# Rebuilding the opening of a fused attention and mixture-of-experts kernel

## The chip, the cores and the metric

The kernel runs on one core of a Trainium2 chip. The metric is the device time of one execution in microseconds (us), the median of several runs. Times inside an execution come from one profiled execution and count from the start of its span.

## What is computed

Causal attention over 8 batches with 8 heads of 576 positions and 64 dimensions, with a bias from a cumulative sum of `max(s, 0)`; its output, as 4608 rows of 512, goes through a layer of eight experts, one expert for each row, chosen by cosine similarity.

```python
scores = q @ k.T / sqrt(64)                       # per batch and head
cum    = cumsum(maximum(s, 0))
scores = where(causal, -1e9, scores + minimum(-(cum[:, None] - cum[None, :]), 0))
attn   = softmax(scores);  o = attn @ v
x      = o as [4608, 512]
e      = argmax(normalize(x) @ normalize(expert_emb).T / tau);  g = softmax(...)[e]
out    = g * (relu(x @ w1[e]) @ w2[e])
```

## The kernel before

The 64 heads are numbered n = 0 to 63, in groups g of four (`HG`) and batches of eight. All instructions are placed by hand, in program order, on each engine's own in-order queue; the only order between engines is what data and buffers demand. `step(n)` places one head's turn.

A softmax needs the maximum of each row ahead of the exponential. The kernel gets it from a first, rougher product: TensorE computes scores with `smax_mm` (1600 columns a head), VectorE takes the maxima. That work is in four parts: `s1` (tile i = 3, 448 columns), `s2` (tiles 2 and 1, 320 and 192), `s3` (half of tile 4, 288) and `s4` (the other half and tile 0, 288 and 64), with the reductions `sr(n, 3)`, `sr(n, 2)`, `sr(n, 1)`, one inside `s3` and two inside `s4`. In the steady state the same work has the names `s1`, `sa`, `s3`, `sb`. Its PSUM tiles are two banks named `s` (`ps_s`, two buffers); each allocation takes the other one, and has to wait until the one before on that bank has been read. Heads below 4 take theirs from `ps_t` for `s1` and `s2`.

The maxima of two heads (`MP`, 128 x 10) become a row: `mrow2` transposes them on TensorE, VectorE negates and shifts them, and a DMA on SyncE's queue (`send`) writes them into row 96 of the group's Q tile `qkb`. `mrow1` only queues that for the next step's pop of `rq`. With that row in place the exact scores need no subtraction.

The exact scores of head n go into two PSUM tiles, `ta` (placed by `ta_`) and `tb` (by `tb_` and `tbl`), by a high product (`hh_`, line 452) and a low one (`hl_`, line 456). The low one reads `QC` and `KC`, which hold for each head what is left of q and k after rounding: `neg` (line 324) and `hcopy` (line 318) on ScalarE write a negated and a plain copy of `qkb`, each for two heads, and `addl` (line 332) adds the unrounded values with an accumulating DMA on POOL's queue. `expa` and `expb1` (ScalarE, lines 489 and 492) take the exponentials; `pl_` (POOL, line 246) makes their low halves `PL`.

V is transposed by `emm` (line 293) through one PSUM tile of one buffer, and split into a high half on ScalarE (`vcp`, line 303) and a low half on VectorE (line 304). `vsq` (line 274) and `vscale` find V's scale for a batch. `pv(n)` (lines 517 to 519) multiplies the probabilities of head n with V two steps later, and `norm1` to `norm3` (lines 530 to 542) divide by the row sums a step after that. The experts follow behind head 63.

Loads: `load(g)` brings a group's q and k (1216 KB, POOL's queue) into one of three `qkb` tiles, `loadc` its rows of the cumulative sum, `zeros` and `onerows` fill the tile's other rows; `loadt` brings V (SyncE's queue).

The opening: steps -4 to -1 do the maxima of heads 0 to 3 with filler matmuls (`heat`, line 200) between them, steps 0 and 1 score heads 0 and 1 while they do the maxima of heads 4 to 6 (`m = n + LA` with `LA` = 5 from step 1 on), and from step 2 each step does the maxima of head n + 5. `prep(n, k)` gives each step two copies or negations on ScalarE for the next groups.

```python
m = n + LA - (n < 1)              # line 993: the head whose maxima step n does
if n == 0:                        # line 1129
    nc.sync.dma_start(cumd..., chl...)
    loadc(2); setup4(); load(2)
if n == 1:                        # line 1081, cut
    vscale(0); fslot(); ...; emm(0); s1(LA); s2(LA); ...
    vcp(0, False); vcp(0, True); prep(1, True); s3(LA); emm(1); s4(LA); mrow1(LA)
```

Of the kernel before, what the change touches and what calls it, by code (L numbers as in the profile page):

```python
# [110 lines left out]
def main(ctx, tc, qkh, qkc, vtin, s_in, emb, tau, w1h, w2h, out, shared, nb):  # L111
# [33 lines left out]
    chl = P32s[2][0:64, 0:2 * S].rearrange("p (x s) -> p x s", x=2).bitcast(F32R)  # L145
# [25 lines left out]
    def zeros(i):  # L171
        w = (QW + KW) // 4
        for j in range(4):
            nc.gpsimd.memset(qkbs[i][64:128, w * j:w * j + w].bitcast(F32), 0.0)
        onerows(i)
# [80 lines left out]
    def loadc(g):  # L256
        if g == 1:
            for i in range(2):
                nc.gpsimd.dma_start(qkbs[1][64 + i:65 + i, QW:].bitcast(F32), chl[HG:2 * HG, i, :].bitcast(F32))
        elif 1 < g < NGg:  # L260
# [73 lines left out]
    def prep(n, k):  # L334
# [3 lines left out]
        if g == 0:  # L338
            if c == 0:
                neg(1, False, 1 - k)  # L340
            elif c < 3:
                hcopy(1, k, c - 1)
            if c < 3:
                return
# [4 lines left out]
        else:  # L349
            hcopy(g + 1, k, c - 1)  # L350

# [13 lines left out]
    def stile(n, name):  # L365
        if n < LA - 1:
# [69 lines left out]

    def mrow2(j):
# [23 lines left out]
    def ta_(n):  # L461
# [3 lines left out]
        if n > 1:  # L465
            s1(n + LA)
# [525 lines left out]
    def step(n):  # L992
        m = n + LA - (n < 1)
# [4 lines left out]
        if m == 0:  # L998
# [3 lines left out]
            for i in range(2):  # L1002
# [5 lines left out]
                if i == 0:  # L1008
                    load(1)
                    zeros(1)  # L1010
                    loadc(1)
            setup2()
            zeros(2)
        if n < 0 and rq:
            rq.popleft()()
            aq.popleft()()
            for p in range(2):
                loadt(0, pair(p))
        if m == 2:
            setup3()  # L1020
        if m == 3:
            r7s[0]()
        if n == 0:
            neg(1, True, 0)
            neg(1, True, 1)
            addl(1, True)
# [9 lines left out]
        if not live or n < 2:  # L1036
            s1(m)
# [4 lines left out]
        if n == 1:  # L1042
            addl(1, False)
# [5 lines left out]
        if live:  # L1049
            expa(n)  # L1050
            if n != 1:
                prep(n, True)
# [9 lines left out]
        if live:  # L1062
            tb_(n)
        sr(m, 2)
        if n < 2:
# [15 lines left out]
        if n == 1:  # L1081
            vscale(0)
            fslot()
            while tasks:
                slot()
            emm(0)
            s1(LA)
            s2(LA)
            for i in (3, 2, 1):
                sr(LA, i)  # L1090
            vcp(0, False)
            vcp(0, True)
            prep(1, True)
            s3(LA)
            emm(1)
            s4(LA)
            mrow1(LA)
# [385 lines left out]
```

## Time and profile before

| | |
|---|---|
| median of 3 runs | 769.9 us (769.21 to 770.17) |
| the profiled execution | 770.33 us, of which its span 768.3 us |
| TensorE busy | 743.2 us (97%) |
| ScalarE, VectorE, POOL busy | 570.8, 525.1, 383.5 us |
| `ta` of head 0, 3, 9 starts | 21.52, 45.65, 74.96 us |

The page gives shares over the whole span; the opening has other limits than what follows. So the opening is read from the timeline of each engine, where each row is one instruction or a run of equal ones, with its start, its duration and, in brackets, how long the engine stood idle ahead of it and whose work ended that. Durations of neighbouring instructions overlap; where a rate is meant, the distance between starts is taken.

### The profile page before, as it was taken

To read this page: it belongs to the slowest core of one execution; us is meant where nothing else is said; L and a number is where in the kernel's file an instruction comes from. 1 tells how busy PE (TensorE), PEld (TensorE's weight loads), DVE (VectorE), ACT (ScalarE), POOL (GpSimd) and SP (SyncE) were. 2 spreads that over 40 slices of the span, in tenths; PEclk is the share of its full clock that TensorE was granted. 3 is DMA by queue.
4 is the path that set the end of the run, shared out by engine and by line. 5 is a ranking of instruction groups with operands and counts; after the bars stand their busy time and mean duration, and the time that the engine had idled before them with its cause. 6 is when DMAs were issued, how large, how long until landed. Compare 5 with 4: busy or idle time off the path is not lost. (4 is left out here: it accounts for less than half of the span.)

```text
span 768.3 us, 22128 instructions
## 1 busy us (share of the span) xinstructions
PE 743.2 (97%) x8587; PEld 550.2 (72%) x8587; DVE 525.1 (68%) x1794; ACT 570.8 (74%) x1024; POOL 383.5 (50%) x371
## 2 busy tenths in 40 slices
PE   7799999999999999999899999999999999999996
PEld 3599999999999999997464545645655555555564
DVE  7677888888888888889567666655665567645621
ACT  7789999999999999988676877738548578474410
POOL 8957798989899898774622130131221302211002
PEclk9889999999999999999999999999999999999999
DMA  8977879797979798854645965654665756643001
GB/s 157 228 175 146 173 181 206 175 216 167 211 170 214 168 206 176 209 168 156 196 150 178 185 192 168 153 194 112 166 199 114 191 168 174 210 106 88 15 15 57
DMA packets 76965, 125.46 MB, mean 163 GB/s; under 512 B 38981, under 2 KB 39385, under 8 KB 75986
## 3 DMA queue, kind: packets, MB, share of 16 engines
q0 software_dynamic: 20288, 71.07, 39.0%
q1 hardware_dynamic: 56564, 52.84, 25.6%
q8 instruction: 75, 1.23, 0.7%
q14 instruction: 38, 0.31, 0.1%
HBM read 95.38 MB, written 21.49 MB: 152 GB/s over the span
## 5 line engine op out<-in xcount | busy, mean ns | idle before, releaser
L246 POOL TENSOR_TENSOR PL<-P 128x576 f16<-128x576 f32 (+2 forms) x128 | 203.6, 1687 | 26.3 <-ACT P L489 15.5
L852 PEld LDWEIGHTS <-wt 128*128 128x128 f16 x1920 | 113.9, 98 | 87.3 <-issue 3.5
L852 PE MATMUL pxs<-xH,wt 128*128 128x512 f16 (+2 forms) x544 | 156.4, 359 | 1.8 <-PEq L901 1.0
L942 POOL DMA_INDIRECT out<-Kx,xj x39 | 41.5, 1064 | 174.6 <-DVE Kx L941 158.1
L725 POOL DMA_INDIRECT Qx<-xs,idx x41 | 42.5, 1036 | 128.1 <-ACT vjunk L807 74.6
L517 PE MATMUL om<-vh,P 128*128 128x73 f16 x945 | 105.1, 199 | 0.7 <-DVE xt L542 0.4
L518 PE MATMUL om<-vl,P 128*128 128x72 f16 x945 | 104.5, 196 | 0.0
L519 PE MATMUL om<-vh,PL 128*128 128x73 f16 x945 | 104.3, 197 | 0.0
L354 PE MATMUL s<-qkb 96*128 96x288 f32 (+4 forms) x270 | 97.0, 373 | 2.0 <-DVE M L362 1.1
L852 PE MATMUL T<-xH,wt 128*128 128x64 f16 x704 | 97.5, 193 | 0.0
L518 PEld LDWEIGHTS <-P 128*128 128x128 bf16 x960 | 94.7, 99 | 1.4 <-issue 1.0
L517 PEld LDWEIGHTS <-P 128*128 128x128 bf16 x960 | 93.6, 98 | 0.9 <-DVE vl L304 0.7
L519 PEld LDWEIGHTS <-PL 128*128 128x128 f16 x960 | 93.8, 98 | 0.0
L852 PE MATMUL pxs<-xL,wt 128*128 128x512 f16 (+1 forms) x256 | 93.0, 363 | 0.0
L362 DVE CUSTOM_DVE_ANT_0 junk<-s,mS 128x320 bf16<-128x320 f32 (+3 forms) x142 | 73.3, 524 | 5.5 <-PE s L354 3.6
L492 ACT ACTIVATE P<-tb 128x1024 f32<-128x1024 f32 x64 | 65.2, 1019 | 4.7 <-PE tb L459 3.2
L456 PE MATMUL tb<-QC,KC 128*128 128x448 f32 (+3 forms) x256 | 64.6, 311 | 0.0
L843 DVE SCALAR_TENSOR_TENSOR wt<-ring,idx,wt 128x512 f16<-128x512 f32 x80 | 56.7, 745 | 9.4 <-ACT wt L835 9.4
L452 PE MATMUL tb<-qkb 128*128 128x448 f32 (+3 forms) x256 | 61.0, 292 | 0.0
L941 DVE TENSOR_SCALAR Kx<-pxs,xj,idx 128x512 f32<-128x512 f32 x31 | 25.1, 808 | 49.9 <-PE pxs L929 38.3
L835 ACT ACTIVATE wt<-ring,idx 128x512 f16<-128x512 f32 x80 | 53.4, 711 | 7.7 <-DVE idx L822 7.7
L402 DVE CUSTOM_DVE_ANT_0 junk<-s,mS,M 128x288 bf16<-128x288 f32 x64 | 33.1, 517 | 37.0 <-PE s L354 36.3
(289 smaller groups left out, 1992.3 us busy)
## 6 DMA issues: line engine op xcount, KB each, us to landing
qkb<-qkh POOLq DMA_DIRECT2D x15, 1216.0 KB, 9.0
ring<-w2h SPq DMA_DIRECT2D x44, 256.0 KB
ring<-w1h SPq DMA_DIRECT2D x36, 256.0 KB
vT<-vtin SPq DMA_DIRECT2D x28, 320.0 KB
KC<-qkh POOLq DMA_DIRECT2D x15, 576.0 KB, 8.7
QC<-qkh POOLq DMA_DIRECT2D x15, 576.0 KB, 7.9
rw<-w1h SPq DMA_DIRECT2D x15, 256.0 KB
rw<-w2h SPq DMA_DIRECT2D x12, 256.0 KB
```

The source lines that it names most:

```text
L246: nc.gpsimd.tensor_tensor(out, a, b_, op=ALU.subtract)
L354: nc.tensor.matmul(out, G[g]["QB"][0:96, h, 128 * i:128 * i + 128], G[g]["KB"][0:96, h, lo:hi], start=True, stop=True)
L362: nc.vector.tensor_tensor_reduce(out=jk, in0=src, in1=ms, scale=1.0, scalar=NEG, op0=ALU.add, op1=ALU.max, accum_out=MP[n // 2][:, n % 2, ...
L452: nc.tensor.matmul(out, G[g]["KB"][:, h, ks:ks + 128], G[g]["QB"][:, h, 64 + qlo:64 + qhi], start=start, stop=False)
L456: nc.tensor.matmul(out, HD[n]["KC"][:, ks:ks + 128], HD[n]["QC"][:, qlo:qhi], start=False, stop=stop)
L492: nc.scalar.activation(HD[n]["P32"][:, 576:1600], HD[n]["tb"], AF.Exp, scale=0.125)
L517: nc.tensor.matmul(out, lh, vh[:, kb], start=(kb == 0), stop=False)
L518: nc.tensor.matmul(out[:, u:u + 72], lh, vl[:, kb], start=False, stop=False)
L519: nc.tensor.matmul(out, ll, vh[:, kb], start=False, stop=(kb == j))
L835: nc.scalar.activation(h, a, AF.Copy, scale=s)
L843: nc.vector.scalar_tensor_tensor(l, a, s, h, op0=ALU.mult, op1=ALU.subtract)
L852: nc.tensor.matmul(o, w[:, 128 * c:128 * c + 128], x[:, c, a:b], start=(c == 0 and k == 0), stop=(c == 3 and k == 2))
```

## The change

- The first row of maxima (heads 0 and 1) is no longer sent by a DMA. `row0` negates and shifts the maxima on VectorE, transposes them column by column on TensorE (ten times 128 x 1) into one PSUM partition, and three copies on ScalarE write them to row 96 of the tile. A DMA of two elements from the same maxima is placed on SyncE's queue ahead of V's load.
- `scores(0, 2)` and `scores(1, 3)` place the exact scores and exponentials of heads 0 and 1 between the maxima of heads 2 and 3; then come the maxima of heads 4 and 5 with filler matmuls (`rows`). `step` begins again with head 2, which also holds the V preparation of heads 0, 1 and 2.
- From step 2 to 8 the maxima follow a table (`MAXIMA`): head 6 in step 2, 7 in step 3, none in step 4, and heads 8 to 13 in halves, three a step, in steps 5 to 8. From step 9 on a step does head n + 5 again.
- The copies and negations of steps 2 to 8 follow a table (`EARLY`). `vsq` of batch 1 moves from steps 2 to 5 to steps 5 and 6, V's load of batch 1 into step 3. `addl(2, ...)` moves from the ends of steps 4 and 5 to those of 5 and 6.
- Q's addition for group 1, `addl(1, False)`, stands ahead of `load(2)` on POOL's queue, both now in step 2; `zeros(2)` stands later on that queue, in two halves around `addl(1, True)`.
- The cumulative sums `chl` lie in the second V tile, and group 2's rows of it are read from there directly.

The diff, without its unchanged lines:

```diff
@@ -145 +145 @@
-    chl = P32s[2][0:64, 0:2 * S].rearrange("p (x s) -> p x s", x=2).bitcast(F32R)
+    chl = vTs[1][0:64].rearrange("p a c -> p (a c)")[:, 2 * CAP:2 * CAP + 2 * S].rearrange("p (x s) -> p x s", x=2).bitcast(F32R)
@@ -171 +171 @@
-    def zeros(i):
+    def zeros(i, js=range(4)):
@@ -173 +173 @@
-        for j in range(4):
+        for j in js:
@@ -175 +174,0 @@
-        onerows(i)
@@ -257 +256 @@
-        if g == 1:
+        if 0 < g < 3:
@@ -259,2 +258,2 @@
-                nc.gpsimd.dma_start(qkbs[1][64 + i:65 + i, QW:].bitcast(F32), chl[HG:2 * HG, i, :].bitcast(F32))
-        elif 1 < g < NGg:
+                (nc.gpsimd if g == 1 else nc.sync).dma_start(qkbs[g][64 + i:65 + i, QW:].bitcast(F32), chl[HG * g:HG * (g + 1), i, :].bitcast(F32))
+        elif g < NGg:
@@ -338,7 +336,0 @@
-        if g == 0:
-            if c == 0:
-                neg(1, False, 1 - k)
-            elif c < 3:
-                hcopy(1, k, c - 1)
-            if c < 3:
-                return
@@ -350,0 +343,28 @@
+
+    def preps(n, k):
+        if n > 8:
+            return prep(n, k)
+        for f, *a in EARLY.get((n, k), ()):
+            f(*a)
+
+    EARLY = {(2, True): ((neg, 1, False, 0), (neg, 1, False, 1)), (3, True): ((hcopy, 1, True, 0),), (3, False): ((hcopy, 1, False, 0),),
+             (4, True): ((hcopy, 1, True, 1),), (4, False): ((hcopy, 1, False, 1),), (5, True): ((neg, 2, True, 0),), (5, False): ((neg, 2, True, 1),),
+             (6, True): ((neg, 2, False, 0),), (6, False): ((neg, 2, False, 1), (hcopy, 2, True, 0)),
+             (7, True): ((hcopy, 2, False, 0), (neg, 3, True, 0)), (7, False): ((neg, 3, False, 0),),
+             (8, True): ((hcopy, 2, True, 1), (neg, 3, True, 1)), (8, False): ((hcopy, 2, False, 1), (neg, 3, False, 1))}
+    MAXIMA = {2: ((0, 6), (1, 6)), 3: ((0, 7), (1, 7)), 5: ((0, 8), (1, 8), (0, 9)), 6: ((1, 9), (0, 10), (1, 10)),
+              7: ((0, 11), (1, 11), (0, 12)), 8: ((1, 12), (0, 13), (1, 13))}
+
+    def early(n, i):
+        if n in MAXIMA and i < len(MAXIMA[n]):
+            half, m = MAXIMA[n][i]
+            if half:
+                s3(m)
+                s4(m)
+                mrow1(m)
+            else:
+                s1(m)
+                sr(m, 3)
+                s2(m)
+                sr(m, 2)
+                sr(m, 1)
@@ -366 +386 @@
-        if n < LA - 1:
+        if n < 2:
@@ -436,0 +457,12 @@
+    def row0():
+        mn = p2.tile([128, 2, 5], F32, name="M")
+        nc.vector.tensor_scalar(mn, MP[0], -1.0, 8.0 * PSH * math.log(2.0), op0=ALU.mult, op1=ALU.add)
+        t, u = ps_t.tile([128, 1024], F32, tag="t", name="row"), ps_m.tile([128, 512], F32, tag="m", name="row")
+        for i in range(10):
+            o = t[0:1, 128 * i:128 * i + 128] if i < 8 else u[0:1, 128 * i - 1024:128 * i - 896]
+            nc.tensor.transpose(out=o, in_=mn[:, i // 5, i % 5:i % 5 + 1], identity=ident)
+        for lo, hi, r in ((0, SP, t), (SP, 1024, t), (1024, 2 * SP, u)):
+            nc.scalar.copy(qkbs[0][96:97, lo:hi], r[0:1, lo % 1024:lo % 1024 + hi - lo])
+        MP["ready", 0] = True
+        nc.sync.dma_start(vjunk[0:1, 0:2].bitcast(F32), mn[0:1, 0, 0:1])
+
@@ -465 +497 @@
-        if n > 1:
+        if n > 8:
@@ -993 +1025 @@
-        m = n + LA - (n < 1)
+        m = n + LA if n > 8 else NH if n > 0 else n + LA - 1
@@ -1010,0 +1043 @@
+                    onerows(1)
@@ -1012,15 +1044,0 @@
-            setup2()
-            zeros(2)
-        if n < 0 and rq:
-            rq.popleft()()
-            aq.popleft()()
-            for p in range(2):
-                loadt(0, pair(p))
-        if m == 2:
-            setup3()
-        if m == 3:
-            r7s[0]()
-        if n == 0:
-            neg(1, True, 0)
-            neg(1, True, 1)
-            addl(1, True)
@@ -1036 +1054,2 @@
-        if not live or n < 2:
+        early(n, 0)
+        if not live:
@@ -1042,2 +1060,0 @@
-        if n == 1:
-            addl(1, False)
@@ -1051,2 +1068,5 @@
-            if n != 1:
-                prep(n, True)
+            preps(n, True)
+        if n == 2:
+            addl(1, False)
+            load(2)
+            setup4()
@@ -1063,0 +1084,9 @@
+        if n == 2:
+            vscale(0)
+            fslot()
+            while tasks:
+                slot()
+            emm(0)
+            vcp(0, False)
+            vcp(0, True)
+        early(n, 1)
@@ -1065 +1094 @@
-        if n < 2:
+        if n < 0:
@@ -1081,19 +1110,7 @@
-        if n == 1:
-            vscale(0)
-            fslot()
-            while tasks:
-                slot()
-            emm(0)
-            s1(LA)
-            s2(LA)
-            for i in (3, 2, 1):
-                sr(LA, i)
-            vcp(0, False)
-            vcp(0, True)
-            prep(1, True)
-            s3(LA)
-            emm(1)
-            s4(LA)
-            mrow1(LA)
-        if live and n > 1:
-            emm(n)
+        if live:
+            emm(1 if n == 2 else n)
+            if n == 2:
+                expb1(n)
+                vcp(1, False)
+                vcp(1, True)
+        early(n, 2)
@@ -1113 +1130,3 @@
-        if n < 2:
+        if n == 2:
+            emm(2)
+        if n < 0:
@@ -1123,5 +1142,3 @@
-            expb1(n)
-            if n:
-                vcp(n, False)
-            else:
-                vsq(0, range(4))
+            if n > 2:
+                expb1(n)
+            vcp(n, False)
@@ -1129,5 +1145,0 @@
-        if n == 0:
-            nc.sync.dma_start(cumd.rearrange("x r s -> r x s").bitcast(F32), chl.bitcast(F32))
-            loadc(2)
-            setup4()
-            load(2)
@@ -1135,3 +1147,2 @@
-            prep(n, False)
-            if n:
-                vcp(n, True)
+            preps(n, False)
+            vcp(n, True)
@@ -1146 +1157,4 @@
-        if live and 2 <= c8 < 6 and b1 < nb:
+        if live and n < H:
+            if 5 <= n < 7:
+                vsq(1, range(2 * n - 10, 2 * n - 8))
+        elif live and 2 <= c8 < 6 and b1 < nb:
@@ -1150,2 +1164,3 @@
-        if live and c8 < 4:
-            loadt(b1, c8)
+        if live and (c8 < 4 if n > 7 else n == 3):
+            for p in range(4) if n == 3 else (c8,):
+                loadt(b1, p)
@@ -1157 +1172,3 @@
-        if live and n >= HG and c < 2:
+        if 5 <= n < 7:
+            addl(2, n == 5)
+        elif live and n > 7 and c < 2:
@@ -1216 +1233,63 @@
-    for n in range(1 - LA, NH + 3):
+    def rows(m):
+        s1(m)
+        heat(1)
+        sr(m, 3)
+        s2(m)
+        heat(1)
+        sr(m, 2)
+        sr(m, 1)
+        s3(m)
+        heat(2)
+        s4(m)
+        heat(2)
+        mrow1(m)
+
+    def scores(n, m):
+        s1(m)
+        sr(m, 3)
+        s2(m)
+        sr(m, 2)
+        sr(m, 1)
+        ta_(n)
+        expa(n)
+        s3(m)
+        tb_(n)
+        tbl(n)
+        expb1(n)
+        s4(m)
+        mrow1(m)
+
+    def send():
+        rq.popleft()()
+        aslot()
+
+    for n in (-4, -3):
+        step(n)
+    rq.popleft()
+    row0()
+    for p in range(2):
+        loadt(0, pair(p))
+    scores(0, 2)
+    scores(1, 3)
+    heat(2)
+    send()
+    pl_(0, 0, 576, "p")
+    setup2()
+    pl_(0, 576, 1600, "p")
+    hset(1)
+    r7s[0]()
+    setup3()
+    neg(1, True, 0)
+    neg(1, True, 1)
+    zeros(2, range(2))
+    addl(1, True)
+    zeros(2, range(2, 4))
+    pl_(1, 0, 576, "p")
+    onerows(2)
+    loadc(2)
+    nc.sync.dma_start(cumd.rearrange("x r s -> r x s").bitcast(F32), chl.bitcast(F32))
+    rows(4)
+    vsq(0, range(4))
+    rows(5)
+    send()
+    for n in range(2, NH + 3):
```

## Rows read from the trace of the kernel before

**Rows 1.** The page, busy time of each engine, with its share of the span.

```profile
PE 743.2 (97%) x8587; PEld 550.2 (72%) x8587; DVE 525.1 (68%) x1794; ACT 570.8 (74%) x1024; POOL 383.5 (50%) x371
```

**Rows 2.** Timeline of TensorE: start, duration, both us; masks of `ta` start heads 3, 5, 6, 9.

```profile
45.65 0.28 PE L459 MATMUL ta<-trim,identb 128*128 128x256 bf16 x1
...
55.37 0.27 PE L459 MATMUL ta<-trim,identb 128*128 128x256 bf16 x1
...
58.14 0.39 PE L354 MATMUL s<-qkb 96*128 96x288 f32 x1
...
58.51 0.22 PE L517 MATMUL om<-vh,P 128*128 128x73 f16 x1
...
60.16 0.27 PE L459 MATMUL ta<-trim,identb 128*128 128x256 bf16 x1
...
74.96 0.27 PE L459 MATMUL ta<-trim,identb 128*128 128x256 bf16 x1
```

**Rows 3.** Timeline: the first row's DMA on SyncE's queue, and TensorE's wait for it.

```profile
17.18 0.78 SPq L445 DMA_DIRECT2D qkb<-mr  x1
...
23.56 0.51 PE L452 MATMUL ta<-qkb 128*128 128x256 f32 x2 [1.77 <-DMA qkb<-mr]
```

**Rows 4.** Table by stretch: busy us (instructions) of each engine, granted clock, DMA.

```profile
26.00:28.00 2.00, 2.00 (x11) 1.92 (x10) 1.15 (x6) 0.56 (x1) 2.00 (x4) 0.50 0.97 181
...
36.00:38.00 2.00, 1.59 (x6) 1.46 (x6) 0.59 (x3) 1.68 (x4) 1.03 (x2) 0.50 1.87 252
```

**Rows 5.** Timeline of VectorE: head 1's maxima, the first, fourth and last row.

```profile
13.80 0.62 DVE L362 CUSTOM_DVE_ANT_0 junk<-s,mS 128x448 bf16<-128x448 f32 x1
...
15.03 0.45 DVE L399 TENSOR_REDUCE M<-s 128x1 f32<-128x288 f32 x1
...
16.34 0.08 DVE L362 DVE_READ_ACCUMULATOR2_ANT M<- 128x1 f32 x1
```

**Rows 6.** Four transposes in the timeline; then groups by line and form (busy, mean ns).

```profile
376.77 0.66 PE L758 MATMUL pxm<-ident,Qx 128*128 128x128 f32 x4 [1.36 <-DMA Qx<-xs,idx]
...
L492 ACT ACTIVATE P<-tb 128x1024 f32<-128x1024 f32 x64 | 65.2, 1019 | 4.7 <-PE tb L459 3.2 <-issue 0.6
...
L769 ACT CAST xH<-pxs 128x512 f16<-128x512 f32 x4 | 2.2, 582 | 1.1 <-PE pxs L758 1.1
```

**Rows 7.** Timeline of ScalarE: step 4 from its first exponential to `vsq`.

```profile
51.80 0.63 ACT L489 ACTIVATE P<-ta 128x576 f32<-128x576 f32 x1
52.33 1.15 ACT L324 ACTIVATE KC<-qkb 64x1152 fp32r<-64x1152 f32 x1
53.38 1.01 ACT L492 ACTIVATE P<-tb 128x1024 f32<-128x1024 f32 x1
54.29 0.62 ACT L303 ACTIVATE vh<-V,sc 128x432 f16<-128x432 f32 x1
54.93 1.16 ACT L324 ACTIVATE QC<-qkb 64x1152 fp32r<-64x1152 f32 x1
56.11 0.74 ACT L274 ACTIVATE vjunk<-vT 128x640 bf16<-128x640 f32 x1
```

**Rows 8.** Timeline of VectorE: normalization of one head, and a low half of V.

```profile
46.71 0.18 DVE L534 RECIPROCAL z<-z 128x5 f32<-128x5 f32 x1
46.93 0.53 DVE L542 TENSOR_TENSOR xt<-om,z 128x360 f32<-128x360 f32 x1
...
55.03 0.66 DVE L304 SCALAR_TENSOR_TENSOR vl<-V,sc,vh 128x432 f16<-128x432 f32 x1
```

**Rows 9.** Timeline of TensorE: `s3` of head 5 waits for its tile.

```profile
34.81 0.40 PE L354 MATMUL s<-qkb 96*128 96x288 f32 x1 [0.49 <-DVE M L362]
```

**Rows 10.** DMA issues: KB each, us to landing; one of 57 us, the page's median, one of 30 us.

```profile
QC<-qkh POOLq DMA_DIRECT2D x1, 576.0 KB, 7.7
...
KC<-qkh POOLq DMA_DIRECT2D x15, 576.0 KB, 8.7
...
qkb<-qkh POOLq DMA_DIRECT2D x1, 1216.0 KB, 10.2
```

## The prediction

> **What bounds the kernel now.** I read the busy table first. TensorE is busy for 743.2 of 768.3 us [rows 1], so every microsecond taken off or put on TensorE's order in the opening reaches the end, unless something later absorbs it. The starts of `ta` say where the opening stops: from head 3 at 45.65 us a head takes about 4.9 us (3 to 9: 29.31 us for six heads) [rows 2]. The part of a step up to its last score matmuls takes 2.77 us (55.37 to 58.14), those matmuls 0.37, the products with V 1.65 (58.51 to 60.16) [rows 2]. Before 45.65 us TensorE has gaps. What costs most there shows in the timeline and in the table by stretch: 1.77 us until the row of maxima for heads 0 and 1 has landed [rows 3], and stretches at half the clock, 1.2 GHz, as in 26 to 28 and 36 to 38 us, the first of them behind that idle time [rows 4].
>
> After step 9 the changed kernel has the old one's state (five heads of lead, the same queues of preparation). The comparison is therefore one number: when does `ta` of head 9 start? Before: 74.96 us [rows 2].
>
> **The change, part by part.** Up to the end of head 1's maxima (16.42 us [rows 5]) nothing on TensorE, VectorE or ScalarE moves.
>
> *Row 0.* Removed: the DMA issued at 17.18 us, which `ta` of head 0 waited for until 23.56 us [rows 3]. Added: one small VectorE operation, ten one-column transposes, three copies on one partition, and a DMA that only holds SyncE. Four transposes take 0.66 us [rows 6], so ten take about 1.5 (bounds 1.0, as their stationary side is one column, and 2.7 if they don't overlap). A copy of 512 columns takes 0.58 us and one of 1024 1.02 [rows 6], so 640 columns take about 0.69, and the first copy can start behind the fifth transpose. Scores of head 0 start at about 18.5 us, five earlier.
>
> *Heads 0 to 5, to the start of step 2.* Here VectorE paces. One head's maxima take it 2.62 us: 1.23 for `s1` and `s2`, 1.39 for `s3` and `s4` [rows 5]. Heads 2 and 3: 5.24 us from 18.6, plus some 1.9 of waits, because `s4` stands behind `ta`, `tb` and `tbl` in TensorE's order: 25.7. Then the row of heads 2 and 3, the router's small copies and `setup3`, 1.9: 27.6. Heads 4 and 5: 5.24 and some waits: 33.0. Their row is transposed and `ta` of head 2 starts at 33.3. The row DMA of heads 2 and 3, issued at 26.7, lands by 33.1 even at the old 6.4 us.
>
> *Step 2.* It holds the V preparation of heads 0, 1 and 2, one after the other through one PSUM tile. ScalarE: the first exponential 0.53 and two negations, 1.18 each between starts [rows 7], until 36.9; then the high half of V (0.62, 37.5), on VectorE the low half (0.66, 38.2) [rows 8], `emm(1)`, its high half (39.3); VectorE still has head 6's maxima until 39.6, then the low half (40.1), `emm(2)` 0.65, and the rest of the products 0.9. That is 41.8. TensorE is idle for 1.65 and 0.9 us in it, much as in the idle time of rows 3, behind which the clock fell [rows 4]; the 1.5 us of V and product matmuls left by then would take twice as long, so a drop costs 0 to 1.5 us, and I take 0.5. Head 3 starts at **42.3 instead of 45.65: 3.3 us gained**.
>
> *Steps 3 to 8.* But the lead is shorter: head 6 is done, where before it was head 7. Heads 7 to 13 now fall into six steps (head 7 in step 3, none in step 4, one and a half per step in 5 to 8), where before it was six heads in six. In work for TensorE that is one head: 544 of its 1600 columns take 0.37 us [rows 2], so about 1.1. It is not what counts. The two score tiles are shared by all six allocations of such a step, and TensorE waits in order for VectorE to have read the tile two allocations back. The trace has that wait once, 0.49 us at 34.81 [rows 9]. In step 5: `s1(8)` follows `ta`, so VectorE starts 1.14 us into the step; 1.23 of reductions; 0.65 for the normalization that stands between (0.18 and 0.53, overlapping) [rows 8]; 1.39 for the second half. Only at 4.5 may `s2(9)` be issued, where TensorE by itself would be there at about 3.3. Then 0.2 and 1.5 of products: 6.2 us. Step 6 the same with the halves exchanged, 6.15. Step 7, 6.35, as its row adds a transpose. In step 8 the row of heads 12 and 13 is transposed in the step that finishes head 13 (`mrow1` is called by `early`, ahead of the pop), so TensorE waits until about 6.0 and then has 0.9 left: 6.9. For the same reason step 3 is 5.65, not 4.8. Step 4, without maxima, is bounded by ScalarE: 0.53 + 1.05 + 0.91 + 0.55 + 1.18 = 4.2 [rows 7].
>
> *Preparation on ScalarE.* Steps 2 to 8 hold 18 negations and copies, where before they held 14, at 1.05 to 1.18 us. The two pairs of `vsq` (0.74 each [rows 7]) stand in steps 5 and 6. Step 6 comes to 7.1 us, so ScalarE ends it 2.5 us into step 7; steps 7 (5.2) and 8 (6.5) hold it there. TensorE has about 2 us of slack to ScalarE (the second exponential of head 4 ends at 54.4 [rows 7], its tile is needed again about a microsecond after `ta` of head 5, at 56.4), so this alone costs nothing. It makes one thing late: Q's addition for group 2 is issued behind the negations of step 6, 6.1 us into it, and `ta` of head 8, in which it is read, starts 12.5 us into it. Landing takes 7.7 us for Q's transfer of group 2 now, and 8.7 in the median of K's [rows 10]. K's addition is a whole step ahead and out of the way, so I take 7.4: it lands at 13.5, 0.6 us behind the 12.85 at which it is read. Bounds: 0 (it isn't behind) and 2.5 (8.7, and ScalarE half a microsecond later).
>
> The Trainium skill ("DMA: Bandwidth & Descriptors", section "Anatomy of one DMA — SWDGE (gpsimd) path") gives a DMA a fixed 2.0 us plus its bytes over 436 GB/s. By that this 576 KB transfer would take 2.0 + 1.35 = 3.4 us (an estimate), and the wait would be nothing, 0.6 us off the sum. The accumulating transfers of the trace take twice that, and I go by them.
>
> *Free.* The third load, behind Q's additions on POOL's queue, is issued at about 38 and lands at 48 to 50 with the 10.2 us of the old one [rows 10]; head 8 needs it in step 5, at 52. Q's additions for group 1 land at 45 and are read at 48. The memsets of `zeros(2)` move behind the first `PL` on POOL; nobody waits for them but the loads. If ScalarE's negations in step 2 were 3 us later, both covers would be gone, at 1 to 2 us.
>
> *Sum.* 42.3 + 5.65 + 4.2 + 6.2 + 6.15 + 6.35 + 7.5 (6.9 + 0.6) = 78.35 us against 74.96: **3.4 us slower**. The profiled execution took 770.33 us, 0.43 over the median of 769.9: 773.7, or 773.3 beside the median.
>
> **The rivals.**
>
> *The lead is built for nothing (faster).* If VectorE's reductions hide behind TensorE in steps 5 to 8, as they do now, a step there costs 4.8 (55.37 to 60.16) plus half a head, 5.3, and step 3 costs 4.8: 4.8 + 4.2 + 4 x 5.3 = 30.2, head 9 at 72.5, 2.5 us earlier: 767.4 (766.9 without the clock's drop). It decides at 5.9 us a step, where it ends level. For it: nothing before shows VectorE holding TensorE in a steady step. Against: its work in such a step is already 3.93 + 0.65 + 0.6 = 5.2, and TensorE's order leaves it idle for about a microsecond at each step's start. The Trainium skill ("Perfetto Trace Analysis", section "Optimization Strategy") says that the same gap repeating can mean too little PSUM for the next tile; by that rule this rival falls. No run so far shows the gap repeating.
>
> *Gain and loss cancel.* The opening as far as head 3 comes out at 41 and the late steps at 5.8 with no wait for Q's addition: about 34 us, 75.0: 769.9.
>
> *The opening doesn't do what it says.* If the clock stays at half from 28.8 (rows of heads 4 and 5 with their filler matmuls: 3.9 us of TensorE against 2.62 of VectorE, 2.6 for the two) and through step 2 (1.5), or if V or a row lands late, head 3 starts at 45.6 as before and the late steps cost as above: 7 us, 777.
>
> **How the numbers follow.** Forecast 0.50, first rival 0.20, cancelling 0.15, late opening 0.15. The measurement can tell about 0.2%, 1.5 us. Faster: the first rival and the lower side of the second, 0.21; same: most of the second and the forecast's lower edge, 0.21; slower 0.58. The forecast's own range is 771.5 to 775.5; the range takes in cancelling and most of the late opening, with a late Q addition (plus 1.9): 768.0 to 777.5.
>
> **What the profile will show.** Head 0's `ta` at 18 to 19 us, head 2's at about 33, head 3's at 42 to 43. In steps 5 to 8 idle time of TensorE ahead of score matmuls (line of `smax_mm`) with VectorE as releaser, about 1 us a step, steps of 6 us or more; in step 8 a wait of the row's transpose. A wait of `ta` of head 8 for Q's addition. After head 9 steps of 4.8 to 5.1 as before. I am wrong if steps 5 to 8 keep to 5.3, or if head 3 starts before 40.

## The result

The changed kernel takes 778.71 us (median of 4 runs, 777.26 to 780.48) where the kernel before takes 770.03 on the same chip (4 runs, 769.21 to 770.72): a ratio of 1.0114, with a 95% interval of 1.0091 to 1.0137. It is 8.7 us slower. The prediction said slower, by 3.4 us; the time lies above its range. One run of experiment 11 (785.99 us, at a granted clock of 0.948 where the other eleven have 0.997 to 0.999) is left out of its ratio.

The profiled execution took 780.48 us, of which its span is 778.4. The one number to which the prediction reduced the change is the start of `ta` of head 9. In the timeline of TensorE of the changed kernel (start, duration, both us; the masks of heads 0, 2, 3, 5, 6, 7, 8 and 9):

```profile
18.48 0.29 PE L491 MATMUL ta<-trim,identb 128*128 128x256 bf16 x1
...
35.74 0.27 PE L491 MATMUL ta<-trim,identb 128*128 128x256 bf16 x1
44.53 0.27 PE L491 MATMUL ta<-trim,identb 128*128 128x256 bf16 x1
...
54.44 0.27 PE L491 MATMUL ta<-trim,identb 128*128 128x256 bf16 x1
60.70 0.27 PE L491 MATMUL ta<-trim,identb 128*128 128x256 bf16 x1
70.28 0.38 PE L491 MATMUL ta<-trim,identb 128*128 128x256 bf16 x1
78.18 0.27 PE L491 MATMUL ta<-trim,identb 128*128 128x256 bf16 x1
85.04 0.27 PE L491 MATMUL ta<-trim,identb 128*128 128x256 bf16 x1
```

Head 9 starts at 85.04 instead of 74.96 [rows 2], 10.1 us later, and the span is 10.1 us longer (778.4 against 768.3). From head 9 to the end both take 693.3 us: everything happens ahead of head 9. Against the forecast of 78.35, the 6.7 us that are missing lie in three places: the start of step 2 (35.74, forecast 33.3), step 6 (9.58, forecast 6.15) and step 7 (7.90, forecast 6.35); the other steps together are 0.7 under the forecast, so the three come to 7.4.

The waits of TensorE in the first 90 us (line that waited, releaser: us in total, times, longest us; the one at L199 is a filler matmul in the first microseconds; L374 is `smax_mm`, L382 the reduction of a score tile, L292 `emm`, L303 V's low half, L463 `row0`, L472 the transposition of a row):

```profile
PE s L374 <- DVE M L382: 3.8, 7, 1.7
PE om L199 <- DVE PL L163: 2.9, 1, 2.9
PE om L277 <- ACT vjunk L273: 2.7, 1, 2.7
PE V L292 <- DVE vl L303: 1.8, 2, 1.3
PE row L463 <- DVE M L459: 1.5, 1, 1.5
PE pm L472 <- DVE M L382: 1.2, 3, 0.5
```

Of the seven waits of the first line four fall into steps 5 to 8:

```profile
56.85 0.43 PE L374 MATMUL s<-qkb 96*128 96x288 f32 x2 [0.29 <-DVE M L382]
58.83 0.50 PE L374 MATMUL s<-qkb 96*128 96x320 f32 x2 [0.22 <-DVE M L382]
63.13 0.50 PE L374 MATMUL s<-qkb 96*128 96x320 f32 x2 [0.34 <-DVE M L382]
80.61 0.50 PE L374 MATMUL s<-qkb 96*128 96x320 f32 x2 [0.35 <-DVE M L382]
```

The wait at L277 is not in the prediction at all. That line is `vscale`: it takes the sums of squares that `vsq` (ScalarE, line 273) has made and reduces them by a matmul, at the end of step 6. In the timeline of ScalarE, and in that of TensorE (the bracket is the idle time ahead, and who ended it):

```profile
65.86 1.17 ACT L323 ACTIVATE QC<-qkb 64x1152 fp32r<-64x1152 f32 x1
66.94 1.13 ACT L317 CAST KC<-qkb 64x1152 fp32r<-64x1152 f32 x1
68.09 0.74 ACT L273 ACTIVATE vjunk<-vT 128x640 bf16<-128x640 f32 x1
...
68.95 0.74 ACT L273 ACTIVATE vjunk<-vT 128x640 bf16<-128x640 f32 x1
69.59 0.19 ACT L273 ACTIVATION_READ_ACCUMULATOR vjunk<-vT 128x1 f32 x1
```

```profile
69.83 0.59 PE L277 MATMUL om<-sq,ones 128*128 128x4 f32 x2 [2.75 <-ACT vjunk L273]
```

The change moved the second pair of squares into step 6, behind two negations and a copy, and left `vscale` at that step's end. So all that ScalarE is late with becomes a wait of TensorE, 2.75 us. In the kernel before, the same matmul (there line 278) finds batch 1's last squares done at 61.87 and doesn't wait. For batch 0, whose squares came directly ahead of it, it did:

```profile
32.66 0.38 PE L278 MATMUL om<-sq,ones 128*128 128x4 f32 x2 [1.13 <-ACT vjunk L274]
...
65.07 0.36 PE L278 MATMUL om<-sq,ones 128*128 128x4 f32 x2
```

The table by stretch (length, then busy us and instructions of PE, PEld, DVE, ACT, POOL, then the granted clock of TensorE, DMA share, GB/s) shows the other two places:

```profile
26.00:28.00 2.00, 1.26 (x8) 0.75 (x7) 1.83 (x6) 2.00 (x3) 1.70 (x3) 1.00 1.02 200
28.00:30.00 2.00, 1.03 (x4) 0.64 (x4) 1.90 (x9) 1.94 (x6) 2.00 (x3) 0.53 0.40 60
30.00:32.00 2.00, 2.00 (x9) 1.17 (x7) 0.83 (x5) 0.93 (x4) 1.92 (x3) 0.50 1.03 169
32.00:34.00 2.00, 2.00 (x8) 1.22 (x7) 1.72 (x7) 0.00 (x0) 1.99 (x4) 0.50 0.70 138
34.00:36.00 2.00, 1.73 (x10) 0.98 (x9) 0.88 (x6) 0.00 (x0) 1.32 (x1) 0.76 0.61 136
...
68.00:70.00 2.00, 0.17 (x1) 0.17 (x2) 0.00 (x0) 1.73 (x5) 2.00 (x3) 0.77 0.54 69
70.00:72.00 2.00, 2.00 (x9) 1.96 (x10) 0.23 (x2) 0.28 (x1) 1.38 (x1) 0.50 1.05 185
72.00:74.00 2.00, 2.00 (x8) 1.91 (x8) 1.94 (x8) 2.00 (x3) 1.15 (x1) 0.50 0.24 43
74.00:76.00 2.00, 2.00 (x13) 2.00 (x12) 1.23 (x6) 0.91 (x2) 0.56 (x1) 0.52 0.00 0
```

The clock is at half, 1.2 GHz, while the maxima of heads 4 and 5 are made (28 to 35 us), and again for most of step 7, directly behind the wait for the squares (TensorE busy for 0.17 of the 2 us from 68 to 70).

### The profile page after: what moved, and what is told of

Read it like the earlier page. It is cut to its first block, busy times and chain, and to the rows that moved or that the text cites. A ratio compares the mean times of both kernels' runs of the same rounds, so it can differ in the third digit from the quotient of the medians.

```text
span 778.4 us, 22149 instructions
## 1 busy us (share of the span) xinstructions
PE 748.7 (96%) x8598; PEld 551.9 (71%) x8598; DVE 527.3 (68%) x1794; ACT 572.8 (74%) x1027; POOL 383.7 (49%) x371
## 5 line engine op out<-in xcount | busy, mean ns | idle before, releaser
L374 PE MATMUL s<-qkb 96*128 96x288 f32 (+4 forms) x284 | 97.5, 370 | 5.4 <-DVE M L382 4.8
L382 DVE CUSTOM_DVE_ANT_0 junk<-s,mS 128x448 bf16<-128x448 f32 (+3 forms) x156 | 76.4, 503 | 9.0 <-PE s L374 7.2
L374 PEld LDWEIGHTS s<-qkb 96*128 96x128 f32 x284 | 54.0, 197 | 14.0 <-DVE M L382 10.9
L521 ACT ACTIVATE P<-ta 128x576 f32<-128x576 f32 x64 | 41.2, 644 | 28.3 <-PE ta L488 24.6
```

Source lines behind the costliest of these rows:

```text
L374: nc.tensor.matmul(out, G[g]["QB"][0:96, h, 128 * i:128 * i + 128], G[g]["KB"][0:96, h, lo:hi], start=True, stop=True)
L382: nc.vector.tensor_tensor_reduce(out=jk, in0=src, in1=ms, scale=1.0, scalar=NEG, op0=ALU.add, op1=ALU.max, accum_out=MP[n // 2][:, n % 2, ...
```

## The experiments

The theory to be tested: the miss is the wait of `vscale` and two falls of the clock; what is left is the tie between VectorE and TensorE that the prediction named. The rival: the wait is only where ScalarE's overload happens to show, and six steps can't build five heads of lead cheaply in any order. Chips differ by half a per cent (the kernel before takes 770.0 to 770.3 us on some and 773.9 on others), so each ratio is against the kernel before on the same chip, and places are compared by the starts of `ta`. On the slower chips (experiments 1 to 4, 9 and 10) the part behind head 9 takes 695.7 to 700.4 us in the profiled executions, elsewhere 692.5 to 693.4; no profile of the kernel before was taken there, so their times say less about the opening than the starts do.

**1. `vscale` a step later.** The squares stay; the matmul that reads them stands in step 7.

```diff
+        if n == 7:                     # behind emm(7)
+            vscale(1)
+            fslot()
-        if live and c8 == 6 and b1 < nb:
+        if live and c8 == 6 and b1 < nb and n > 6:
```

> The changed kernel, but the sum that vscale takes on TensorE for batch 1 stands behind emm in step 7 instead of at the end of step 6. Theory (TensorE waits 2.75 us in step 6 for the two squares of vsq that the change moved into the same step, and the clock then falls to half for 6.8 us): steps 6 and 7 go from 9.6 and 7.9 us to about 6.4 each, the time falls by 4 to 5 us, to about 774. Rival (ScalarE is overloaded in steps 5 to 8 and would hold TensorE in any case, here or at the next tile): under 1.5 us gained, the wait reappears ahead of tb of head 7 or ta of head 8.

Step 6 fell from 9.58 to 6.22 us (58.85 to 65.07), near the prediction's 6.15. Step 7 took 7.45: a new wait of 0.80 us stands in it, of the products with V for the scale (`sc`) that now is made too late, and no drop of the clock. Head 9 started at 79.39. The time was 781.18 us, ratio 1.0085 (1.0063 to 1.0106). So the wait was that of this reader, and moving it cost 0.8 back. The time fell by much less than the 4 to 5 us expected: 7.3 us over the kernel before instead of 8.5 to 8.7, which by the time alone is the rival's sign (under 1.5 us). Head 9 starts only 2.4 us earlier than in experiment 5, the changed kernel without a fall of the clock in the opening, and the part behind it takes 700.4 us. What decides against the rival is experiment 10.

**2. More filler matmuls in the opening.** Nine more between the maxima of head 4 and three ahead of the row of heads 2 and 3.

```diff
-        heat(1)                        # between s1 and s2
+        heat(4 if m == 4 else 1)
-        heat(1)                        # behind s2
+        heat(7 if m == 4 else 1)
-    heat(2)                            # ahead of the first send()
+    heat(5)
```

> The changed kernel with 12 more filler matmuls in the stretch of 24.5 to 29 us, where TensorE idles for 1.7 us ahead of s3 of head 4. Theory (the granted clock falls to half at 28.2 us behind that idle time, and the maxima of heads 4 and 5 then cost 3.3 and 3.5 us each instead of 2.6): clock 1.00 from 28 to 35 us, ta of head 2 starts about 2 us earlier, at 33.5 to 34, and the time falls by 2 us. Rival (VectorE paces those rows whatever the clock): ta of head 2 stays at 35 to 36, no gain.

The clock stayed at 1.00 from 26 to 40 us and head 2 started at 34.00 instead of 35.74. But the granted clock fell later, in step 2 (0.80 in 40 to 42, 0.50 in 42 to 44), and step 2 took 10.20 instead of 8.79. Step 6 waited as before (9.38). In step 7 the clock did not fall this time, and it took 6.37, near the prediction's 6.35. Time 781.38, ratio 1.0091 (1.0073 to 1.011): about a microsecond gained of the 2 expected, as the fall only stood elsewhere.

**3. Both.**

> Both of the edits above. If they are the two terms that the prediction missed, they add: 778.7 - 4.7 - 2.1, about 772, within 1.5 us of the 773.3 of the prediction, and head 9 starts at about 78. Rival (the two share a cause, or DMA lands later than the earlier work needs it): 774 to 776.

The clock stayed at 1.00 from 26 to 80 us; head 2 at 33.83, steps 3 to 8 of 5.43, 4.50, 6.26, 6.23, 7.45 and 6.87 us, head 9 at 79.37. Time 779.04, ratio 1.0058 (1.0039 to 1.0078). The forecast had 33.3, then 5.65, 4.2, 6.2, 6.15, 6.35 and 7.5, and head 9 at 78.35. With the wait at `vscale` and the clock's falls gone, head 9 starts 1.0 us behind the forecast. By time the two edits did not add up as expected: 5.2 us over the kernel before, 3.3 to 3.5 less than the changed kernel, where 6.8 were expected. 4.4 of the 5.2 stand in the start of head 9 (74.96 before, on another chip).

**4. Shorter reductions.** On top of 3, the reductions of heads 8 to 13 in the tiles 3, 2 and 1 read only the last 128 columns, and those in the first half of tile 4 only 64 (its second half and tile 0 stay whole): part of the maxima is left out, to make VectorE faster with all else in place.

```diff
+        if 7 < n < 14 and i:
+            src, w = src[:, w - 128:w], 128
```

> As the one with both edits, but for heads 8 to 13 VectorE takes the maxima over the last 128 columns of each tile (64 of the first half of the last one) instead of all: that part of the maxima is left out. TensorE's work is the same. Theory (in steps 5 to 8 TensorE waits for VectorE to have read the score tiles): VectorE's maxima fall from 2.6 to about 1.8 us a head, the four steps from 6.2 to about 5.2 each, 3 to 4 us less than with both edits alone. Rival (TensorE or ScalarE paces these steps): no change beyond 0.5 us.

Steps 5 to 8 took 5.46, 5.75, 6.37 and 7.40 us, 24.98 together against 26.81 in experiment 3. The 1.8 us show that VectorE's reading does set TensorE's pace there, and they are less than the 3 to 4 expected: step 8 got longer by 0.5 us. In it VectorE starts the first reduction (72.34) only behind a wait of 1.38 us for V's high half on ScalarE, and the low product of head 8 starts 0.66 us behind the high one instead of 0.35. The one buffer (`mr`) for the rows shows in the step behind it: VectorE waits 1.75 us, until 78.43, for the row before to be sent, and step 9 takes 5.33 us instead of 4.69. Time 778.12, ratio 1.0053 (1.0031 to 1.0075), 0.9 us under experiment 3, which these intervals don't tell apart.

**5. The changed kernel again**, on another chip.

> The changed kernel once more, on the chip of this call, to be compared with the three beside it. Theory: vscale waits in TensorE's order in step 6 (9.4 to 9.6 us) and the opening falls to half the clock somewhere; head 9 starts 8 to 10 us later than the 74.96 of before, and the median is 7.5 to 9.5 us over the kernel before of the same chip. Rival (the loss is chance of one chip): under 4 us.

778.82 against 770.31, ratio 1.0113 (1.0096 to 1.013). Its profiled execution, 777.22 us, had no fall of the clock in the opening and only a short one behind step 6: head 2 at 33.67 instead of 35.74, step 6 9.38, step 7 6.86 instead of 7.90, head 9 at 81.76 instead of 85.04. The 3.28 us between these starts are the 3.26 us between the two executions' times. So what differs between these two is the clock, 2.1 us in the opening and 1.2 in steps 6 and 7. The wait of 2.75 us is in both, and in the profile of experiment 2. The table of experiment 5, with the granted clock third from the end; behind step 6 it is low from 68 to 72 us only:

```profile
28.00:30.00 2.00, 1.20 (x7) 0.70 (x8) 1.80 (x9) 1.91 (x7) 2.00 (x3) 1.00 0.58 68
30.00:32.00 2.00, 2.00 (x10) 0.97 (x8) 1.92 (x9) 0.74 (x2) 1.92 (x2) 1.00 0.94 161
...
68.00:70.00 2.00, 2.00 (x11) 1.96 (x11) 0.80 (x5) 0.88 (x2) 1.48 (x2) 0.61 1.06 197
70.00:72.00 2.00, 2.00 (x10) 1.91 (x9) 1.85 (x9) 1.87 (x2) 0.99 (x1) 0.53 0.35 63
```

**6. The first row alone.** The kernel before with `row0` in place of its first row's DMA, nothing else.

```diff
-            rq.popleft()()
-            aq.popleft()()
+            rq.popleft()
+            row0()
```

> The kernel before with only the first row of maxima built by TensorE and ScalarE; all else in its old order. If the row's DMA was a stall on the path that sets the end: ta of head 0 starts at 21.6 instead of 23.56 and the whole gains 1 to 2 us. Theory: the gain does not get through, since the maxima of head 4 that follow then wait for the rows of group 1, which land at 24.3; ta of head 0 near 21.6, head 3 at 45.0 to 45.6, and the median 0 to 0.6 us under the kernel before.

769.49 us, ratio 0.9987 (0.9975 to 0.9999). In the profile nothing is gained: `ta` of head 0 starts at 23.81, not at the 21.6 expected, and its first product at 23.84 (23.56 before); head 3 at 45.74, head 9 at 75.04 (45.65 and 74.96 before). The wait of 1.77 us [rows 3] is gone, but the ten transposes and their wait for VectorE now stand ahead of the maxima of heads 2 and 3, and the maxima of head 4 wait longer than the 0.57 us of before:

```profile
25.86 0.68 PE L354 MATMUL s<-qkb 96*128 96x448 f32 x3 [1.25 <-POOL qkb L174]
```

The releaser named, a memset, is hardly the cause: the `qkb` tile that this matmul reads was filled with zeros by 16.5 us. In the kernel before it waited for the DMA of group 1's rows; here that isn't shown. Where the 0.8 us of the median come from, the profile doesn't show either. Of all kernels here it is the fastest, by an interval that just excludes no gain.

**7. Two negations earlier.** On top of 3, the negations for group 1 that stood behind the first exponential of step 2 go ahead of the maxima of head 5, where ScalarE was idle.

```diff
-    EARLY = {(2, True): ((neg, 1, False, 0), (neg, 1, False, 1)), ...
+    EARLY = {...
+    neg(1, False, 0)                   # ahead of rows(5)
+    neg(1, False, 1)
```

> e3 (vscale moved to step 7, more filler matmuls in the opening) with the two negations that stand in ScalarE's order behind the first exponential of head 2 put ahead of the rows of heads 4 and 5, where ScalarE is idle. Theory: step 2 hangs on ScalarE's order and VectorE's reductions alike; without the negations it is about 0.7 us shorter (8.1 instead of 8.8), the rest as in e3. Rival (VectorE's maxima of head 6 set step 2 alone): step 2 stays at 8.8. If ScalarE's order set all of it: 2 us shorter.

Step 2 took 8.13 us instead of 8.80, as expected, and head 9 started at 78.69. Time 773.56 against 770.31, ratio 1.0044 (1.0027 to 1.0061); the four runs lie between 773.52 and 774.45, at a mean clock of 0.998 to 0.999. 3.25 us over the kernel before is near the forecast of 3.4, with its mechanism and without the wait at `vscale` or the clock's falls; that it is so near is partly luck, as the shorter step 2 (0.67 us) and the wait for `sc` left in step 7 (0.80), neither of them in the forecast, nearly cancel.

**8 and 9. The order rearranged.** Experiment 2's filler matmuls; the router's small copies directly behind the first row; the work of 7 and Q's addition with the third load ahead of the maxima of head 5; the first pieces of the maxima in step 4 instead of step 5; each row transposed a step later; the negations spread anew; V's load of batch 1 in step 2 and `addl(2, ...)` a step earlier; the second pair of squares early in step 6. Experiment 9 sends the row of heads 6 and 7 in step 3 again. The diff, cut:

```diff
-    MAXIMA = {..., 5: ((0, 8), (1, 8), (0, 9)), 6: ((1, 9), (0, 10), (1, 10)),
-              7: ((0, 11), (1, 11), (0, 12)), 8: ((1, 12), (0, 13), (1, 13))}
+    MAXIMA = {..., 4: (None, (0, 8), (1, 8)), 5: ((0, 9), (1, 9)), 6: ((0, 10), (1, 10), (0, 11)),
+              7: ((1, 11), (0, 12)), 8: ((1, 12), (0, 13), (1, 13))}
+            if n == 6:                 # behind the first copy
+                vsq(1, (2, 3))
-        if live and (c8 < 4 if n > 7 else n == 3):
+        if live and (c8 < 4 if n > 7 else n == 2):
-            for p in range(4) if n == 3 else (c8,):
+            for p in range(4) if n == 2 else (c8,):
                 loadt(b1, p)
```

> The changed kernel rearranged: filler matmuls as in e2; the router's small copies, the two negations, the V additions of group 1 and the third load ahead of the rows of heads 4 and 5; the maxima of head 8 in step 4, which has none; each row transposed a step later; the negations and copies spread anew; the two pairs of squares in step 5 and early in step 6, so that vscale at the end of step 6 does not wait. Theory (the loss is the uneven spread of the maxima and three waits, all of order, not of work): head 9 starts at 73 to 76, and the median is 2 us under to 1 us over the kernel before. Rival (six steps cannot take six heads of maxima by VectorE beside the products in any order): step 4 takes what steps 5 to 8 give back, head 9 at 78 or later, 3 us or more over.

> e8 with the row of heads 6 and 7 sent in the step that finishes head 7 (step 3), as in the changed kernel, not a step later; in e8 ta of head 6 waited 2.57 us for it and TensorE fell to half the clock behind that. Theory: step 3 grows by 0.3, step 6 falls from 11.5 to 5.7; head 9 starts at 74.5 to 76, and the median is 0.5 us under to 1.5 us over the kernel before. Rival (six steps cannot take six heads of maxima): the wait is only pushed on, head 9 at 78 or later, 3 us or more over.

Steps 3 to 5 came out at 5.33, 5.02 and 5.33 us in experiment 8, but step 6 at 11.52: `ta` of head 6 waited 2.57 us for its row of maxima, and the clock fell to half behind that. Head 9 started at 80.52; 773.88 us, ratio 1.0046 (1.003 to 1.0062). I put it down to the row sent a step later, and that was wrong: with the row sent in step 3 (experiment 9) the wait was 3.05 us. SyncE's queue and TensorE in experiment 9:

```profile
45.99 1.79 SPq L265 DMA_DIRECT2D vT<-vtin  x4
47.88 0.76 SPq L481 DMA_DIRECT2D qkb<-mr  x1
```

```profile
61.16 0.85 PE L488 MATMUL ta<-qkb 128*128 128x256 f32 x2 [3.05 <-DMA qkb<-mr]
```

The row has 5 KB; the four loads of V issued right ahead of it on the same queue, by my own move of `loadt` into step 2, have 320 KB each. It was waited for until 13 us behind its issue. 776.3 against 773.93 us, ratio 1.0031 (1.0019 to 1.0043).

**10. Only the squares earlier.** The changed kernel, with the second pair of squares behind the first negation of step 6 instead of at its end.

> The changed kernel with only the second pair of squares moved, from the end of step 6 to behind the first negation of that step, so that they are done when vscale at the end of step 6 reads them. Theory: the idle 2.75 us ahead of vscale and the clock's fall behind it go, steps 6 and 7 take 6.2 to 6.6 and 6.4 instead of 9.4 to 9.6 and 6.9 to 7.9, 3.5 to 5 us less than the changed kernel: 3.5 to 5 us over the kernel before. Rival (ScalarE's overload, not the place of the squares): step 6 still waits for ScalarE, now for the second exponential or V's high half, and keeps over 8 us.

Step 6 took 6.44 us, step 7 6.37; TensorE did not wait for the squares at all:

```profile
65.79 0.36 PE L277 MATMUL om<-sq,ones 128*128 128x4 f32 x2
```

778.55 against 773.93, ratio 1.0058 (1.0043 to 1.0073): 4.6 us over the kernel before instead of 8.5 to 8.7, and that with the clock at half in part of the opening (0.77 in 28 to 32, 0.81 in 32 to 36, head 2 at 34.60). The rival, that ScalarE's overload would show in another place, falls: ScalarE had the same work, and step 6 is 2.9 us shorter than the shorter of the two in the changed kernel.

It brought out one wait that the changed kernel hides, in the timeline of TensorE in step 8:

```profile
73.48 0.50 PE L488 MATMUL ta<-QC,KC 128*128 128x320 f32 x2 [0.56 <-ACT QC L323]
```

ScalarE's negation, which the profile names because it ended last, is for group 3 and in the other of the two Q tiles; head 8 doesn't read it. What head 8 reads is Q's addition for group 2, issued at 67.38 on POOL's queue, 6.1 us earlier; that the wait is for it is inferred from this. The prediction had a wait of 0.6 us for it.

**11. The row ahead of the V loads.** Experiment 9 with `loadt` back in step 3, behind the row.

```diff
-        if live and (c8 < 4 if n > 7 else n == 2):
+        if live and (c8 < 4 if n > 7 else n == 3):
```

> e9 with the four V loads of the next batch (1280 KB) issued behind the row of heads 6 and 7 on SyncE's queue, as in the changed kernel; in e9 they stood ahead of it, the row was issued at 47.88, and ta of head 6 waited 3.05 us for it until 61.16, 13 us after its issue. Theory (the row lay behind the V loads, and the clock fell behind the wait): the row lands by 55, no wait, step 6 falls from 10.59 to 5.7; head 9 starts at 74.5 to 76, and the median is 0.5 us under to 1.5 us over the kernel before. Rival (the third load's 1216 KB delay the row, whatever stands ahead of it on its queue): the wait stays, at 2 us or more, and with it head 9 at 78 or later.

771.2 us (12 runs) against 770.02, ratio 1.0015 (1.0006 to 1.0025). The row, issued at 46.96 ahead of the V loads at 47.76, was not waited for. The third load stood beside it as before, so the place on the queue decided. What TensorE still waits for in 16 to 90 us (lines 378, 386, 467 and 476 are 374, 382, 463 and 472 of the changed kernel; the longest wait of each kind comes last):

```profile
PE s L378 <- DVE M L386: 2.4, 6, 0.6
PE row L467 <- DVE base L239: 1.6, 1, 1.6
PE V L292 <- DVE vl L303: 1.2, 2, 0.7
PE pm L476 <- DVE M L386: 0.4, 1, 0.4
```

Head 2 starts at 33.78, head 3 at 41.94, head 9 at 76.50; steps 3 to 8 take 5.43, 4.91, 5.33, 6.58, 5.95 and 6.36 us. The rival that no order can do it cheaply falls: the new order with its twelve filler matmuls is worth 7.3 of the 8.5 us. But no order tried here makes the change pay: head 3 comes 3.7 us earlier than before, and heads 3 to 9, with one head more to build, take 5.2 back (34.56 us for heads 3 to 9 against 29.31 [rows 2]).

## Why the prediction was wrong in size and right in direction

*Right.* Row 0: head 0's `ta` at 18.48, forecast 18.5; its ten transposes took 1.25 us (forecast 1.5). Step 2: 8.79 us, forecast 9.0, with two waits for V's low half of 1.29 and 0.54. Steps 3, 4 and 5: 5.43, 4.48 and 6.26, forecast 5.65, 4.2 and 6.2 (the 4.2 has 0.55 us where [rows 7] give 0.64, from 54.29 to 54.93). The mechanism of steps 5 to 8: TensorE waits for VectorE ahead of score matmuls, and each step is 6.2 us or more. The waits are smaller than the 1 us a step of the forecast, 0.29 and 0.22 in step 5; together with the other two of steps 5 to 8 they are 1.2 us, where about 4 were forecast. By experiment 4, which shortened step 5 by 0.80, VectorE's part in its length is larger than its two rows. "The lead is built for nothing" is refuted, since VectorE's reductions did not hide; experiment 4 shows that they carry part of the length. By the rule of the Trainium skill ("Perfetto Trace Analysis", section "Optimization Strategy") on a repeating gap and too little PSUM that rival falls; the trace agrees, with the four waits of 0.22 to 0.35 us in steps 5 to 8.

*The step that failed.* "TensorE has about 2 us of slack to ScalarE (...), so this alone costs nothing." The slack was counted from the exponentials, the only readers of ScalarE that the argument looked at. The prediction moved `vsq` into steps 5 and 6 and counted its cost on ScalarE, but did not ask who reads its result, although the diff left `vscale` at the end of step 6. ScalarE was forecast to end step 6 2.5 us into step 7; TensorE waited 2.75. The size was there, and the reader was missing. The trace of the kernel before had shown this reader waiting once, 1.13 us at 32.66. Experiments 1 and 10 bring step 6 to 6.22 and 6.44 us without touching ScalarE's work.

*The clock.* The prediction gave the drop 0.5 us, in step 2, and had the half clock during the maxima of heads 4 and 5 only in a rival, at 2.6 us for the two. It happened there in the profiled run, at 2.1 us, and was absent from that of experiment 5. Behind the wait for the squares it cost 1.0 us more in the first than in the second, and in the first 1.55 over the forecast. The median lies between the two: about 3 of its 5.3 us over the forecast are step 6 with the wait that all three profiles show (the first, experiments 2 and 5). The rest is, by these profiles, the clock's share that comes and goes; the other runs have no profile.

*A smaller term.* Step 8 was forecast at 7.5 with 0.6 of wait for Q's addition; it took 6.86, as the addition had been covered by the long steps 6 and 7. In experiment 10, without these, the wait is 0.56 and step 8 7.66. Two errors cancelled there: the addition was issued 7.8 us into step 6 (67.38 behind 59.57), where the forecast had 6.1, and was there at most 6.1 us later, where the forecast had 7.4; in the changed kernel the landing took 5.8 (the median of two). The Trainium skill's formula ("DMA: Bandwidth & Descriptors", section "Anatomy of one DMA — SWDGE (gpsimd) path") gives 3.4 us, an estimate; the runs are nearer to the old rows' 7.7 [rows 10].

*What the sum would have been.* Experiment 3, without the wait at `vscale` and without the clock's falls, has head 9 at 79.37, forecast 78.35. Each term is within 0.65 us of the forecast except step 7, 7.45 instead of 6.35, which holds the wait of 0.80 us for `sc` that the moved reader brought in. Experiment 7, with step 2 0.67 us shorter besides, is 3.25 us slower; the forecast was 3.4.

## What to carry to other kernels

When work is moved on an engine that runs late, list the readers of each result that it makes, not the readers of its usual products: the engine's lateness costs nothing until one reader in another engine's order stands at the wrong place. A lead that is to be built over several steps was cheaper here when its work was spread more evenly over them, the step with none of it included (experiment 11 against 7); and what is saved ahead of the build is worth only what the build leaves of it. A small transfer that is waited for goes ahead of the large ones on its queue.

## What had not been expected of the hardware

A VectorE operation of 8 columns took seven times as long beside POOL's memset. In the changed kernel the router's cast stands on the way to the maxima of head 4. POOL and VectorE there:

```profile
25.50 2.15 POOL L174 MEMSET qkb<- 64x1216 f32 x2
```

```profile
26.62 1.07 DVE L239 CAST base<-ebase 128x8 f32<-128x8 int32 x1
```

The two memsets end at 27.65, the cast at 27.69. In experiments 3 and 7 it started at 26.74 and 26.51 and took 0.94 and 1.18 us, so it ended at 27.68 and 27.69 again; in experiment 8, where it stands at 16.59 with no memset beside it, it took 0.16. In experiments 5 and 10 it started at 26.40, in the first of the two memsets, and ended with that one (25.51 + 1.11 = 26.62); the next operation, a TENSOR_SCALAR of 0.17 us in the changed kernel, was held in its place:

```profile
26.40 0.24 DVE L239 CAST base<-ebase 128x8 f32<-128x8 int32 x1
26.68 1.04 DVE L240 TENSOR_SCALAR wsel<-base 128x8 f32<-128x8 f32 x1
```

In all these profiles, then, the operation that came beside a memset ended with one of the two, the first or the second: it waits, and the two engines do not run side by side more slowly. The Trainium skill ("SBUF — State Buffer", section "🔬 SBUF: two separate sides") describes a port pair that GpSimd shares with some of VectorE's operations and that one of the two holds for a whole instruction; these rows agree. On the path that sets the end it was worth little: head 2 starts at 33.65 in experiment 8 and at 33.84 in experiment 7.

The same idle time doesn't always bring the clock down. In the four profiles with the changed opening TensorE stood idle for 1.6 to 1.8 us ahead of about 29 us; the clock fell behind that in the changed kernel (idle 1.71 us) and in experiment 10 (1.76), and stayed at 1.00 in experiments 1 (1.63) and 5 (1.75). In none of the seven profiles with more filler matmuls there did it fall before head 2, though in experiment 2 it fell in step 2.
